# A decode transformer block on one core: coarser score steps, PV first in TensorE's loop, fewer loads at the end, wider down tiles

## The chip, the core and the metric

One core of a Trainium2 chip runs the whole block as one program. The metric is device time in microseconds (us), the median of several executions. The profile is one execution; its span is some 1.2 us shorter than that execution's device time (201.7 against 202.93 before). Engines are written as the profile writes them: PE is TensorE, PEld its weight loads, DVE VectorE, ACT ScalarE, SPq the queue that issues the loads. TensorE's clock is full or half in these traces; "cold" means half.

## The reference, cut to what matters

```python
# x: (1,1,640)  k_cache, v_cache: (1,32,4096,128)  wq: (640,4096)  wo: (4096,640)   all bf16
def A(x):                                  # 32 heads of 128, one query token
    q = (x @ wq) per head
    p = softmax(q . K^T / sqrt(128))       # 4096 keys a head
    return (p . V) @ wo
def B(x):                                  # gated GELU, inner width 1728
    return (gelu(x @ w_gate) * (x @ w_up)) @ w_down
h  = x + A(layernorm(x))
h2 = h + B(layernorm(h))
```

There is one token, so every weight and every cache entry is used once: 84.2 MB must come in from memory for one row of output.

## The kernel before

The heads run in 8 groups of 4. For each group K and V come in as loads of 4 MB. DVE multiplies K by the query, in four steps of 32 rows, TensorE adds up the products over 8 slices of 16 by matmuls with an identity matrix (a "fold"), and DVE adds the last 16 columns in PSUM, the memory that TensorE's results go to in these traces. TensorE's loop puts the product of probabilities and V ("PV") of the group before between the third and the fourth fold:

```python
    def fold(e, i):                        # one step of 32 rows: 8 matmuls of 512 columns into one bank
        for b in range(8):
            mm = held if b else lambda e, *a, **k: e.matmul(*a, **k)
            r = mm(e, ps_f[i % 2][:, :], id_b[:, :], prod[:, i, :, 16 * b:16 * b + 16], start=(b == 0), stop=(b == 7))
    ...
    lp = P.loop("tensor", range(1, NG), [
        ("h", lambda e, k: head_sum(e, k * 4 - 4), lambda k: [evs[k - 2] if k > 1 else qc], False),
        body_fold(0), body_fold(1), body_fold(2),
        ("pv", lambda e, k: pv(e, view(v_slot), range(32)), lambda k: [blocks[k - 1], landed["V"][k - 1][0]], True),
        body_fold(3)])
```

There is one buffer for V, so the next V may be asked for only when PV has read the last. At the end each load is cut so that work can start on its first part:

```python
    wo_load("0", 0, 0, 16)
    wo_load("1a", 1, 0, 12)
    wo_load("1b", 1, 12, 16)
    ...
    proj_part(0, 0, 16, ap, d_wo["0"])     # 160 matmuls of one column in all, in three parts
    proj_part(1, 0, 12, ap, d_wo["1a"])
    pr = proj_part(1, 12, 16, d_wo["1b"])
    ...
    # gate and up: 14 tiles of w, at step 4; the fourteenth has 64 columns
    ws = w[:, c, 512 * (m // 4) + m % 4:512 * (m // 4) + 512:4] if m < 12 else w[:, c, 128 * m:min(128 * m + 128, DF)]
    ...
    # down: four outputs of 160 columns, at partitions 0, 32, 64 and 96
    i = e.matmul(ps_d[32 * q:32 * q + 1, 0:160], h, wd_sb[:, m, n:n + 160], start=False, stop=(m == 11))
```

The softmax here doesn't subtract the row's maximum and nothing guards it: scores larger than these inputs give would overflow.

## Time and profile before

| | before |
|---|---|
| time, median of the first 3 runs | 203.23 us (202.88 to 203.44) |
| span of the profile | 201.7 us |
| moved by the loads | 84.31 MB, mean 418 GB/s |
| PE, DVE busy | 60%, 52% of the span |
| last load landed (trace) | 199.40 us |

### The profile page before, as it was taken

What the parts mean: (1) busy time and instruction counts of PE and PEld (TensorE: products, weight loads), DVE (VectorE), ACT (ScalarE), POOL (GpSimd) and SP (SyncE); (2) the same over time, 40 slices, a digit from 0 to 9 for tenths busy, and PEclk for the clock granted to TensorE, in tenths of its full rate; (3) what the DMA queues carried; (4) which work ended last, traced back from release to release, by engine and by line L of the source; (5) the groups of instructions that cost most, each with busy time, mean ns of one, the idle gap of its engine ahead of it and who ended that gap; (6) DMA issues with size and microseconds to landing.
All of it is one profiled execution on the core that took longest, in us unless ns stands there. A gap on an engine that the chain in (4) does not pass through costs nothing.

```text
span 201.7 us, 2059 instructions
## 1 busy us (share of the span) xinstructions
PE 121.9 (60%) x1002; PEld 36.9 (18%) x778; DVE 105.7 (52%) x114; ACT 12.6 (6%) x33; POOL 2.4 (1%) x8
## 2 busy tenths in 40 slices
PE   0108057759566907880896198528834894777395
PEld 0103000201200300030012001200120013467383
DVE  4200189898189328924890589069707963000221
ACT  2100000000100100010001000100100010100101
POOL 4000000000000000000000000000000000000000
PEclk9999859988979985995589679966985698555555
DMA  9999999999999999999999999999999999999992
GB/s 357 415 398 468 429 422 416 422 442 465 377 455 422 422 422 444 429 455 422 422 422 435 442 429 442 429 422 416 448 429 448 393 432 427 427 408 440 409 411 105
DMA packets 4329, 84.31 MB, mean 418 GB/s; under 512 B 482, under 2 KB 868, under 8 KB 1508
## 3 DMA queue, kind: packets, MB, share of 16 engines
q1 hardware_dynamic: 4322, 84.23, 97.9%
q8 instruction: 4, 0.07, 0.1%
q14 instruction: 1, 0.01, 0.0%
q10 hardware_dynamic: 2, 0.00, 0.0%
HBM read 84.23 MB, written 0.00 MB: 418 GB/s over the span
## 4 chain that ended last, share of the span: by engine, by line
DMA 60%; DVE 20%; PE 11%; SPq 6%; ACT 1%; issue 1%
DMA k_slot<-in_A_k_cache_dram 49%; DVE prod L377 15%; DMA k_slot<-in_B_w_down_dram 11%; SPq L59 6%; PE bank L167 6%; PE bank L353 4%; DVE sc L369 3%; DVE p_bd L394 1%; PE bank L346 1%; ACT pt L392 1%; PE bank L521 0%; DVE out_row L534 0%
## 5 line engine op out<-in xcount | busy, mean ns | idle before, releaser
L377 DVE TENSOR_TENSOR prod<-k_slot,qb 128x4096 bf16<-128x4096 bf16 x32 | 73.0, 2285 | 43.4 <-DMA k_slot<-in_A_k_cache_dram 43.4
L167 PE MATMUL bank<-prod,id_b 128*128 128x512 bf16 x224 | 66.7, 448 | 0.0
L346 PE MATMUL bank<-prod,id_b 128*128 128x512 bf16 x32 | 14.9, 465 | 53.3 <-DVE prod L377 53.0
L369 DVE TENSOR_REDUCE sc<-bank 128x32 f32<-128x512 f32 x32 | 21.9, 686 | 3.8 <-PE bank L167 3.8
L346 PEld LDWEIGHTS bank<-prod,id_b 128*128 128x128 bf16 x32 | 3.1, 98 | 102.5 <-DVE prod L377 99.5
L353 PE MATMUL bank<-v_slot,p_bd 128*16 128x512 bf16 x224 | 13.3, 379 | 0.0
L359 PEld LDWEIGHTS bank<-hs,po_sb 128*128 128x128 f32 x72 | 10.2, 207 | 13.3 <-issue 10.0
L359 PE MATMUL bank<-hs,po_sb 128*128 128x4 f32 x72 | 9.5, 255 | 0.7 <-ACT po_sb L366 0.7
L366 ACT COPY po_sb<-bank 128x512 f32<-128x512 f32 x8 | 4.7, 586 | 73.0 <-PE bank L353 73.0
L332 PE MATMUL bank<-arena,xlnB 128*32 128x512 bf16 x40 | 4.5, 630 | 7.0 <-DMA arena<-in_A_wq_dram 7.0
L491 PE MATMUL bank<-hlnT,v_slot 128*128 128x1 bf16 (+1 forms) x140 | 6.7, 176 | 3.0 <-DMA v_slot<-in_B_w_gate_dram 3.0
L353 PEld LDWEIGHTS bank<-v_slot,p_bd 128*16 128x16 bf16 x224 | 5.0, 89 | 17.6 <-issue 12.8
L394 DVE TENSOR_TENSOR p_bd<-pt,own 128x512 bf16<-128x512 bf16 x8 | 5.5, 693 | 4.5 <-ACT pt L392 4.5
L448 PE MATMUL bank<-aP,arena 128*128 128x1 bf16 x160 | 6.7, 178 | 1.9 <-DMA arena<-in_A_wo_dram 1.9
L392 ACT ACTIVATE pt<-sc,zero_t 128x128 bf16<-128x128 f32 x8 | 3.2, 402 | 71.7 <-DVE sc L369 71.7
L491 PEld LDWEIGHTS bank<-hlnT,v_slot 128*128 128x128 bf16 (+1 forms) x140 | 6.3, 118 | 3.9 <-DVE hX L481 3.1
L448 PEld LDWEIGHTS bank<-aP,arena 128*128 128x128 bf16 x160 | 6.6, 131 | 2.0 <-DMA arena<-in_A_wo_dram 1.3
L336 DVE CAST qb<-bank 128x512 bf16<-128x512 f32 x1 | 0.7, 692 | 10.0 <-PE bank L332 10.0
L306 PE MATMUL bank<-one_bf,x_row 1*128 1x1 bf16 x5 | 0.4, 177 | 7.1 <-DMA x_row<-in_A_x_dram 7.1
L478 DVE TENSOR_TENSOR hT<-xx,bank 128x5 f32<-128x5 f32 x1 | 0.2, 161 | 8.3 <-PE bank L448 8.3
L353 PE MATMUL bank<-k_slot,p_bd 128*16 128x512 bf16 x32 | 2.9, 502 | 1.2 <-DMA k_slot<-in_A_v_cache_dram 1.2
L432 DVE TENSOR_TENSOR aT<-bank,rz 128x32 bf16<-128x32 f32 x1 | 0.2, 192 | 6.3 <-PE bank L359 6.3
(68 smaller groups left out, 28.0 us busy)
## 6 DMA issues: line engine op xcount, KB each, us to landing
k_slot<-in_A_k_cache_dram SPq DMA_DIRECT2D x8, 4096.0 KB, 25.5
v_slot<-in_A_v_cache_dram SPq DMA_DIRECT2D x7, 4096.0 KB, 16.1
arena<-in_A_wq_dram SPq DMA_DIRECT2D x1, 5120.0 KB, 15.4
k_slot<-in_A_v_cache_dram SPq DMA_DIRECT2D x2, 2048.0 KB, 22.9
arena<-in_A_wo_dram SPq DMA_DIRECT2D x1, 2560.0 KB, 30.7
v_slot<-in_B_w_gate_dram SPq DMA_DIRECT2D x1, 2160.0 KB, 24.6
arena<-in_A_wo_dram SPq DMA_DIRECT2D x1, 1920.0 KB, 34.8
v_slot<-in_B_w_up_dram SPq DMA_DIRECT2D x1, 1296.0 KB, 27.3
```

The costliest lines, as they stand in the source:

```text
L59: ev = self.op(eng, lambda e: e.dma_start(out, in_), *deps, dma=True, chan=chan)
L167: built = e.matmul(out, lhsT, rhs, start=start, stop=stop)
L346: mm = held if b else lambda e, *a, **k: e.matmul(*a, **k)
L353: i = e.matmul(ps_o[a:a + 16, :], p_bd[:, 4 * b:4 * b + 4, :].rearrange("p g j -> p (g j)"), vt[:, 4 * b:4 * b + 4, :], start=(b < 4), sto ...
L359: i = e.matmul(ps_a[:, bass.ds(at, 4)], po_sb[:, 128 * r:128 * r + 128], hs[:, r, :], start=(r == 0), stop=(r == 3))
L366: evs[G] = AS(lambda e: e.copy(po_sb[:, :], ps_o[:, :]), pvs[G])
L369: reds[4 * G + i] = VS(lambda e: e.reduce_sum(sc[:, G % 2, 32 * i:32 * i + 32], ps_f[i % 2][:, :].rearrange("p (g d) -> p g d", d=16), axi ...
L377: mults[s] = VS(lambda e, i=i: e.tensor_tensor(out=prod[:, i, :, :], in0=kt[:, 32 * i:32 * i + 32, :], in1=qb[:, G, :].unsqueeze(1).to_bro ...
L392: exps[G] = AS(lambda e: e.activation(pt[:, G % 2, :], sc[:, G % 2, :], ACTF.Exp, bias=zero_t[:, 0:1], scale=INV_SQRT_DH, accum_out=RS[:, ...
L394: blocks[G] = VS(lambda e: e.tensor_tensor(out=p_bd[:, :, :], in0=pt[:, G % 2, :].unsqueeze(2).to_broadcast([128, 128, 4]), in1=own[:, :]. ...
L448: r = e.matmul(ps_p[:, c:c + 1], wo_sb[:, t, i, c::5], aP[:, t, i:i + 1], start=(t == 0 and c == 0 and i == 0), stop=(t == 1 and i == 15), ...
L491: i = e.matmul(ps[0:128 if m < 13 else 64, m:m + 1], ws, hlnT[:, c:c + 1], start=(c == 0 and m == 0), stop=(c == 4), skip_group_check=True)
```

## The change

Its intent is fewer and larger pieces: half as many products, a quarter as many sums, one load each for wo and up, no duplicate selection tables, two output tiles instead of four. The core of the diff, with cuts:

```diff
-    prod = sb("prod", [128, 4, 32, DH], BF16)
+    prod = sb("prod", [128, 2, 64, DH], BF16)
+    ps_f = psum[:, 0:2048]
...
+        reds[G] = VS(lambda e: e.reduce_sum(sc[:, :], ps_f.rearrange("p (g d) -> p g d", d=16), axis=AX.X),
+                     folds[G, 1], exps.get(G - 1))
...
     lp = P.loop("tensor", range(1, NG), [
-        ("h", ...), body_fold(0), body_fold(1), body_fold(2), ("pv", ...), body_fold(3)])
+        ("pv", lambda e, k: pv(e, view(v_slot)), lambda k: [blocks[k - 1], landed["V"][k - 1]], True),
+        body_fold(0), body_fold(1),
+        ("h", lambda e, k: head_sum(e, k * 4 - 4), lambda k: [evs[k - 1]], False)])
...
-    wo_load("0", 0, 0, 16)
-    wo_load("1a", 1, 0, 12)
-    wo_load("1b", 1, 12, 16)
+    d_wo = P.dma("sync", wo_sb[:, :, :], A_wo[:, :].rearrange("(p i) n -> p i n", i=32), qd)
...
-    d_wu = [P.dma("sync", wu_sb[:, 0:3, :], wu_v[:, 0:3, :]),
-            P.dma("sync", wu_sb[:, 3:5, :], wu_v[:, 3:5, :])]
+    d_wu = P.dma("sync", wu_sb, B_w_up[:, :].rearrange("(p c) n -> p c n", c=5))
+    blk = {0: (0, 7), 7: (896, 6)}
...
+                    lo, per = (0, 7) if m < 7 else (896, 6)
+                    at, step = (lo + m - 7 * (m >= 7), per) if m < 13 else (1600, 1)
+                    i = e.matmul(ps[:, m:m + 1], w[:, c, at:at + 127 * step + 1:step], hlnT[:, c:c + 1],
...
+    tiles = ((0, 280), (280, 360))
+                        i = e.matmul(ps_d[32 * t:32 * t + 1, o:o + w], hc, wd_sb[:, m, a:a + w], start=False, stop=(m == 12))
```

Besides these, setup moves from DVE to GpSimd, the Q projection changes its order, the last V comes as one load with its PV in one piece (before, two halves), and x is added to the attention's result by a matmul.

## The prediction

> **What bounds the kernel now.** I read the busy slices of the page first, then the chain that ended last, then the queue's own waits, then the timeline of one group and of the last 32 us.
>
> ```profile
> PEclk9999859988979985995589679966985698555555
> DMA  9999999999999999999999999999999999999992
> ```
>
> The DMA row is full from the first slice to the last but one: 84.31 MB at a mean of 418 GB/s. TensorE is at half clock for the last six slices.
>
> ```profile
> 176.75 22.26 DMA k_slot<-in_B_w_down_dram
> 199.01 0.04 issue
> 199.05 0.74 PE bank L521 x13
> 199.80 0.30 DVE out_row L534
> ```
>
> The chain ends in the last load. Only 2.7 us of the 201.7 follow it, so before is bound by bytes, and TensorE's tail is hidden just barely. The queue's own waits say whether loads are issued late:
>
> ```profile
> SPq L59 <- PE bank L353: 104.1, 6, 18.6
> SPq L59 <- DVE prod L377: 49.9, 2, 34.1
> ```
>
> These waits fill the issuer's time but not the engines': in the timeline of one group
>
> ```profile
> 93.64 2.29 DVE L377 TENSOR_TENSOR prod<-k_slot,qb 128x4096 bf16<-128x4096 bf16 x1 [6.89 <-DMA k_slot<-in_A_k_cache_dram]
> ...
> 104.67 1.90 PE L353 MATMUL bank<-v_slot,p_bd 128*16 128x512 bf16 x32
> ...
> 106.62 0.33 SPq L59 DMA_DIRECT2D v_slot<-in_A_v_cache_dram  x1
> ...
> 113.06 2.29 DVE L377 TENSOR_TENSOR prod<-k_slot,qb 128x4096 bf16<-128x4096 bf16 x1 [6.70 <-DMA k_slot<-in_A_k_cache_dram]
> ```
>
> the next V is issued at 106.62 while the K that lands at 113.06 is still moving: 6.4 us of slack. One group lasts 19.42 us = 8.39 MB at 432 GB/s. The tail, TensorE:
>
> ```profile
> 169.16 1.04 PE L353 MATMUL bank<-k_slot,p_bd 128*16 128x512 bf16 x16
> 171.43 1.89 PE L353 MATMUL bank<-k_slot,p_bd 128*16 128x512 bf16 x16 [1.23 <-DMA k_slot<-in_A_v_cache_dram]
> ...
> 177.63 3.33 PE L448 MATMUL bank<-aP,arena 128*128 128x1 bf16 x80 [0.72 <-DMA arena<-in_A_wo_dram]
> ...
> 182.15 3.36 PE L448 MATMUL bank<-aP,arena 128*128 128x1 bf16 x80 [1.18 <-DMA arena<-in_A_wo_dram]
> ...
> 189.60 3.34 PE L491 MATMUL bank<-hlnT,v_slot 128*128 128x1 bf16 x70 [3.04 <-DMA v_slot<-in_B_w_gate_dram]
> 192.87 0.71 PE L500 MATMUL bank<-hX,ones_f 128*1 128x160 f32 x8
> 193.51 3.37 PE L491 MATMUL bank<-hlnT,v_slot 128*128 128x1 bf16 x70
> 197.33 1.50 PE L521 MATMUL bank<-k_slot,hm 128*1 128x160 bf16 x40
> ```
>
> Every stage waits for its own load and half of the output projection is done before the rest of wo lands. That is why 16 us of TensorE work fit behind the loads.
>
> **What the Trainium skill says.** (1) "DMA: Bandwidth & Descriptors", section "Where 436 GB/s comes from": 435 GB/s is the ceiling of the ports. The trace agrees (432 in the stream), so the stream has nothing to give. (2) "TensorE: Matmul & The Clock Gate", "The HAM clock gate": the clock halves after an idle window of about 3.4 us and comes back after about 3.4 us of activity. The trace agrees in the stream (half clock at the start of each group), but from 189.6 to 196.9 TensorE ran one-column matmuls without a gap and stayed at half clock: such work does not wake it. So I count the tail at half clock. (3) Same page, "Weight-path perf modes": fast weight load needs 128 weight columns. It agrees: equal 0.66 us windows hold 17 matmuls of the projection (40 ns each) but only 14 of the gate, since each 14 of those have one tile of 64 columns; the 13 full tiles come 33 ns apart, so the 64-column one costs some 0.23 us. (4) "SBUF — State Buffer", note on cachelines of 16 bytes: at least two hits per line are needed for full speed. The trace fits: weights at step 4 (two hits) come every 33 ns, at step 5 every 40 ns. In TensorE cycles of 1/1.2 ns that is 40 and 48, so my estimate is 8 + 8 x step: 56 cycles (47 ns) at step 6, 64 (53 ns) at step 7.
>
> **The change, part by part.**
>
> *Stream (K and V).* DVE: four products of 2.20 and four sums of 0.60 a group become two products (2.20 x 2 = 4.4, same rate) and one sum of 2048 columns ((2048/512) x 0.533 + 0.15 = 2.3); 11.9 us a group becomes 11.8, so nothing. What moves is order. PV first means it runs as V lands, 9.7 us after K; in half clock 32 matmuls take 3.6 (16 took 1.89), so V is issued some 13.5 us after K's landing where 13.0 was: slack about 6 us, still no gap. But both folds now stand behind PV: 32 folds of 0.23 us, the first few at 0.43, end 20 to 24 us after K's landing, and sum, exponent and block follow (2.3 + 0.5 + 0.7 + gaps = 3.6). The next group's products slip to 4 to 8 us behind their K, still inside the period of 19.4. The stream stays full: 0 us. Setup moved to GpSimd, and Q projection (pairs in one column group now, up to 9 us for 4.4) end about when the first K lands at 25.1: 0 us.
>
> *End of attention.* K of the last group lands at 151.9. Folds end at 172 to 176 (middle 174), block at 177.5. PV of 32 in one piece 1.9 to 3.6, evacuation 0.7, head sums 1.0 to 1.9, five small steps 1.7: aP ready at 182.6 to 185.2, where it was 177.1. The last V landed at 171.4, and wo's 5.24 MB at 422 GB/s come 12.4 us later, 183.8, now in one load. So the projection starts at about 184.6 (not under 183.9), all 160 matmuls of it: 160 x 0.040 = 6.4. Before, it ended at 185.5; now at 191.2. Lost: 5.7 us. Before had 1.5 us to spare until the gate's load at 189.5, so 4.1 of it comes out as delay there.
>
> *GLU.* Layer norm unchanged (h at 185.54 to first gate matmul possible at 188.0: 2.5). Gate per fifth: 7 x 53 + 6 x 47 + 33 = 0.69 us against 0.66: the 64-column tile goes (-0.2) and the steps 7 and 6 eat it. 3.4 us each for gate and up, about +0.1 each; if steps above 4 cost only 40 ns, 2.6 each, -1.4 in all.
>
> *Residual.* Four column groups of 160 at 4 passes took 0.65 (533 ns + 0.11); two of 280 and 360 take 360 x 4/1.2 = 1.2 + 0.11 = 1.31: +0.66.
>
> *Down.* Four 160-column matmuls side by side came every 133 ns a tile (160/1.2). Two of 280 and 360 take 300 ns. Before, 10 tiles ran from 197.33 and the last four waited for loads; end 199.78. Now all loads (landed by 199.4 as before) are there when the activations are: 14 x 0.30 + 0.24 = 4.4 us, all exposed, against 2.45.
>
> *Output.* One copy of 360 on ACT (0.15 + 360 x 0.85 ns = 0.46) for two of 0.29 in a row (0.62): -0.16.
>
> *Sum, along the new chain:* projection start 184.6; +6.6 to h; +2.5 to gate; +3.3 and 0.14 to the residual; +1.3; +3.2 up; +0.66 to the first down matmul (as before, 196.67 to 197.33); +4.4 to the copy; +0.5; +1.2 to the end of the write (200.5 to 201.7 before). This gives 208.4, against 201.7: +6.7 us. On 203.2 that is 209.9; I take 209.6, since the cheaper GLU would take up to 1.4 off.
>
> **The rivals.** (a) *The loads still end it*: fewer and longer rows (the last slice but three fell to 353 GB/s with 1280-byte rows), one 128-column tile instead of the slow 64-column one, and PV earlier; then nothing moves, 202 to 204. For it: DMA is the bound now. Against: TensorE's tail alone is 24 us from wo's landing (6.6 + 2.5 + 6.9 + 1.3 + 0.7 + 4.4 + 1.7) where the loads leave 15.6. (b) *The stream starves*: the late folds push products and loads so far that the queue runs dry for some us per group; 212 to 220. For it: V's slack is only 6 us, the clock could stay half longer. Against: PV waits for V alone, not for the folds. (c) *Clock*: PV, folds and down keep TensorE warm into the tail; the down stage and the GLU then cost half, 205 to 207. Against: no wake-up from one-column work before. (d) *Folds of the last group all cold*: they end at 179, aP near 190, 214 to 215.
>
> **Range and chances.** Start of projection 183.9 to 186, GLU 2.6 to 3.5 each: 206.9 to 211.5 in time; some weight for (b) and (d) puts the top at 212.0, for (c) the bottom at 207.0. The 2% line is 207.3. Faster by over 2% would need 4 us from a stream at the ports' ceiling: 1%. Within 2%: 13%. Slower: 86%.
>
> **What would show it.** DMA slices still 9 until about 199, then zeros for about 9 us (right) or zeros inside the stream (rival b). The chain should end in TensorE lines: projection, gate, residual, up, down, with no wait for B's loads. Projection near 184.6 and 6.4 long; gate windows at 46 to 54 ns a matmul; down at 300 ns a tile. If the chain still ends in in_B_w_down_dram, or the projection starts before 183.8, I am wrong on the tail; if the clock row shows full speed after 185, on the clock.

## The result, and the profile after

| | before | after |
|---|---|---|
| time, median of 4 runs each, same rounds | 203.33 us (202.88 to 203.64) | 208.92 us (208.54 to 209.06) |
| ratio, with 95% interval | | 1.0274 (1.0249 to 1.0298) |
| span | 201.7 us | 207.3 us |
| packets | 4329 | 3609 |
| last load landed (trace) | 199.40 us | 199.25 us |

A ratio here is the mean time of a kernel's fast runs over that of the other's of the same rounds, so it is not quite the ratio of the medians. The change is slower by 2.7%, close to the 209.6 us predicted.

The busy slices of the page after, to be held against the two rows of before:

```profile
PEclk9999857958965995599559958965896589675557
DMA  9899999999999999999999999999999998999900
```

The loads run as densely as before and stop 8 us before the end (199.25 of 207.3) instead of 2.3. The stream did not slow down; the engines were left behind it. The last part of the chain that ended last (start, duration, what):

```profile
146.89 36.81 DMA arena<-in_A_wo_dram
183.70 0.14 issue
183.84 6.55 PE psum L431 x160
...
192.93 3.57 PE psum L447 x70
196.50 1.30 PE psum L457 x4
197.79 3.51 PE psum L447 x70
...
201.81 3.75 PE psum L482 x25
205.56 0.02 issue
205.58 0.45 ACT out_row L494
```

Before, this chain ended in a load of down weights at 199.0. Now the last load on it is wo, at 183.7, and then come projection (L431), gate (L447), residual (L457), up (L447) and down (L482) one behind the other, none waiting for a load. One group of the stream, from the timeline:

```profile
98.77 8.76 DVE L356 TENSOR_TENSOR prod<-k_slot,qb 128x8192 bf16<-128x8192 bf16 x2
103.55 3.59 PE L343 MATMUL psum<-v_slot,p_bd 128*16 128x512 bf16 x32 [7.49 <-DMA v_slot<-in_A_v_cache_dram]
...
107.19 0.33 SPq L59 DMA_DIRECT2D v_slot<-in_A_v_cache_dram  x1
...
115.26 2.29 DVE L365 TENSOR_REDUCE sc<-psum 128x128 f32<-128x2048 f32 x1 [7.73 <-PE psum L167]
```

PV now runs when V lands (103.55) and cold: 3.59 us for 32 matmuls (1.90 at full clock before). V is asked for at 107.19, while the K that lands at 113.22 is under way: 6.0 us of slack, where before had 6.4. The sum comes 21.5 us after its K landed (93.80 in the trace), as late as expected, and still the loads have no gap. The end of attention, from the same view:

```profile
177.01 3.13 PE L343 MATMUL psum<-k_slot,p_bd 128*16 128x512 bf16 x32 [2.85 <-DVE p_bd L369]
...
183.16 0.19 DVE L406 CAST aP<-psum 128x32 bf16<-128x32 f32 x1 [0.28 <-PE psum L404]
...
183.84 6.53 PE L431 MATMUL psum<-aP,arena 128*128 128x1 bf16 x160 [0.50 <-DMA arena<-in_A_wo_dram]
```

Two things come together at 183.8 in this execution: the attention output aP is ready at 183.35 (177.13 before), and the one load of wo lands at 183.70. Either alone would have stopped the early start of the projection. That they meet within 0.4 us is this execution's: in the profiles of e4, e5 and e6, which leave this part as it is, aP was ready 0.5 to 1.5 us before the load landed. This pair is what the experiments had to take apart.

### The profile page after: what moved, and what is told of

Same layout as the page of the kernel before. It is cut to its first block, busy times and chain, and to the rows that moved or that the text cites. A ratio compares the mean times of both kernels' runs of the same rounds, so it can differ in the third digit from the quotient of the medians.

```text
span 207.3 us, 1891 instructions
## 1 busy us (share of the span) xinstructions
PE 122.0 (59%) x964; PEld 36.8 (18%) x704; DVE 101.3 (49%) x63; ACT 12.4 (6%) x32; POOL 2.1 (1%) x13
## 2 busy tenths in 40 slices
DMA packets 3609, 84.31 MB, mean 407 GB/s; under 512 B 402, under 2 KB 660, under 8 KB 916
## 4 chain that ended last, share of the span: by engine, by line
DMA 77%; PE 20%; DVE 1%; issue 1%; SPq 1%; ACT 1%; DVEq 0%
DMA v_slot<-in_A_v_cache_dram 59%; DMA arena<-in_A_wo_dram 18%; PE psum L343 10%; PE psum L447 3%; PE psum L431 3%; PE psum L482 2%; PE psum L457 1%; SPq L59 1%; PE psum L301 0%; ACT out_row L494 0%; ACT ln L306 0%; ACT ln L305 0%; DVE hlnT L435 0%; DVE ln L303 0%; PE psum L485 0%
## 5 line engine op out<-in xcount | busy, mean ns | idle before, releaser
L356 DVE TENSOR_TENSOR prod<-k_slot,qb 128x8192 bf16<-128x8192 bf16 x16 | 70.0, 4419 | 4.4 <-DMA k_slot<-in_A_k_cache_dram 4.4
L167 PE MATMUL psum<-prod,id_b 128*128 128x512 bf16 x240 | 58.8, 400 | 0.0
L343 PE MATMUL psum<-v_slot,p_bd 128*16 128x512 bf16 x224 | 25.0, 626 | 52.7 <-DMA v_slot<-in_A_v_cache_dram 52.7
L365 DVE TENSOR_REDUCE sc<-psum 128x128 f32<-128x2048 f32 x8 | 18.3, 2292 | 54.1 <-PE psum L167 54.1
L343 PEld LDWEIGHTS psum<-v_slot,p_bd 128*16 128x16 bf16 x224 | 6.9, 124 | 68.7 <-DMA v_slot<-in_A_v_cache_dram 56.9
L336 PE MATMUL psum<-prod,id_b 128*128 128x512 bf16 x16 | 7.3, 454 | 9.6 <-DVE prod L356 9.6
L349 PEld LDWEIGHTS psum<-hs,po_sb 128*128 128x128 f32 x64 | 8.4, 192 | 23.9 <-issue 23.5
L447 PE MATMUL psum<-hlnT,v_slot 128*128 128x1 bf16 x140 | 7.1, 188 | 1.5 <-DVE hlnT L435 1.5
L349 PE MATMUL psum<-hs,po_sb 128*128 128x4 f32 x64 | 7.8, 244 | 0.1
L447 PEld LDWEIGHTS psum<-hlnT,v_slot 128*128 128x128 bf16 x140 | 7.0, 146 | 2.8 <-DVE hlnT L435 1.6
L431 PE MATMUL psum<-aP,arena 128*128 128x1 bf16 x160 | 6.5, 178 | 0.5 <-DMA arena<-in_A_wo_dram 0.5
L431 PEld LDWEIGHTS psum<-aP,arena 128*128 128x128 bf16 x160 | 6.5, 131 | 0.6 <-DVE aP L406 0.6
L482 PE MATMUL psum<-k_slot,hm 128*1 128x280 bf16 (+3 forms) x29 | 3.8, 431 | 0.0
```

Source lines behind the costliest of these rows:

```text
L167: built = e.matmul(out, lhsT, rhs, start=start, stop=stop)
L343: i = e.matmul(ps_o[a:a + 16, :], p_bd[:, 4 * b:4 * b + 4, :].rearrange("p g j -> p (g j)"), vt[:, 4 * b:4 * b + 4, :], start=(b < 4), sto ...
L349: i = e.matmul(ps_a[:, bass.ds(at, 4)], po_sb[:, 128 * r:128 * r + 128], hs[:, r, :], start=(r == 0), stop=(r == 3))
L356: mults[G, i] = VS(lambda e, i=i: e.tensor_tensor(out=prod[:, i, :, :], in0=kt[:, 64 * i:64 * i + 64, :], in1=qb[:, G, :].unsqueeze(1).to_ ...
L365: reds[G] = VS(lambda e: e.reduce_sum(sc[:, :], ps_f.rearrange("p (g d) -> p g d", d=16), axis=AX.X), folds[G, 1], exps.get(G - 1))
L431: r = e.matmul(ps_p[:, c:c + 1], wo_sb[:, i, c::5], aP[:, i:i + 1], start=False, stop=(i == 31), skip_group_check=True)
```

## The experiments

The theory: the stream is unharmed and the 5.6 us come from TensorE's tail behind wo, where every term now counts in full: all of the projection (two gates side by side, the single load and the late aP), the gate and up stages (the weight columns' steps 7 and 6), residual and down (two tiles for four). The rivals: one of the two gates alone, the loads of the tail, or a stream that is delayed by the score steps. Twelve kernels were run, five rounds each except one. "Points" below are percentage points of the ratio to before; one point is 2.03 us. A "gate" here is a wait that holds the projection back; the stage with the weights w_gate is called the gate stage. Where PV comes last, executions differ by more than elsewhere, and a ratio's interval is about 0.25 to 0.5 points to each side.

### e1_wo_parts: open the gate of the load

```diff
-    d_wo = P.dma("sync", wo_sb[:, :, :], A_wo ..., qd)
+    wo_parts = ((0, 16), (16, 28), (28, 32))
+    d_wo = [P.dma("sync", wo_sb[:, lo:hi, :], wo_v[:, lo:hi, :], qd) for lo, hi in wo_parts]
+    for (lo, hi), d in zip(wo_parts, d_wo):
+        pr = proj(lo, hi, ap, d)
```

> The changed kernel with the output projection's weights in three loads (half, three eighths, one eighth) and the projection cut to match; PV stays first in the loop. Theory (two gates side by side: the one load lands at 183.8, but the attention output is ready only at 183.35 because PV stands ahead of the folds): the projection can start only 0.4 us earlier, so 208.5, -0.4 us. Rival (the single load alone is what delays the projection): the first two parts are done under the last load and the time drops by 3 to 4 us, to 205 to 206.

Measured: 208.28 us, ratio 1.0237, so 0.37 points or 0.75 us faster than the changed kernel (0.1 to 1.4 us by the two intervals); the span fell by 0.5. The theory held, the rival did not. The projection starts as soon as aP is there, and all 160 matmuls follow without a wait:

```profile
183.27 6.56 PE L433 MATMUL psum<-aP,arena 128*128 128x1 bf16 x160
```

### e2_pv_last, e3_both and e7_three: open the other gate by moving PV behind the folds

```diff
     lp = P.loop("tensor", range(1, NG), [
-        ("pv", ...),
         body_fold(0), body_fold(1),
+        ("pv", ...),
         ("h", ...)])
```

e3_both adds the three loads of e1_wo_parts, and e7_three the four tiles of e4_down4 as well.

> The changed kernel with PV after both folds in TensorE's loop; the weights of the projection stay one load. Theory: the attention output is ready near 177 instead of 183.35, but the projection still waits for the one load at 183.8: no change, 208.9 within 0.3. Rival (PV first alone is the cause): 3 to 4 us faster, 205 to 206.

> The changed kernel with both edits, the three loads and PV last. Theory: both gates open, the projection ends near 185.5 and the gate projection starts when its own weights land, near 189.1 instead of 192.9: -3.8 us, 205.1. That is far more than the sum of the two single edits (-0.4). Rival (the two are additive): -0.4 or less if both singles do little.

> The changed kernel with the three loads, PV last, and the four-tile residual, down and output: still score steps of 64 rows, one sum over 4 banks, blocks of 7 and 6. Theory: the tail hides behind the loads again, the last load lands at about 199.2 and the time is that of the kernel before, 203.1 within 0.4; the parts left (64 rows, one sum, 7 and 6) cost nothing while the loads are the bound. Rival (the score steps or the sum delay the stream): 204.5 or more.

Measured: 215.16 us (1.0580), 212.59 us (1.0449) and 211.98 us (1.0382). All three expectations missed on the level: the edit itself costs over 6 us. The DMA row of e2_pv_last's page and its queue's timeline say why:

```profile
DMA  9899999998389999999999999999999999989920
```

```profile
56.95 0.33 SPq L59 DMA_DIRECT2D v_slot<-in_A_v_cache_dram  x1
```

The second V was asked for at 48.09 in the changed kernel and is asked for at 56.95 here, because PV of the first group now stands behind both folds of the second. The K under way had landed at 54.4 and the queue ran dry: the next V landed 4.4 us later than in the changed kernel (69.06 against 64.65), and the last V 5.1 later. So the "PV first" of the change is not an ornament: with steps of 64 rows it is what keeps the loads without a gap. I had counted that part as 0 us, which was its net worth in the change, but the change without it would have been far worse.

The comparison of e2 with e3, which share the gap, still tests the gates. In e2 TensorE waits 5.70 us for the one load with its inputs ready:

```profile
188.95 6.21 PE L431 MATMUL psum<-aP,arena 128*128 128x1 bf16 x152 [5.70 <-DMA arena<-in_A_wo_dram]
```

and cutting the load then gives 1.31 points, 2.7 us, where with PV first it gave 0.75. The traces also show what PV's place does to aP: it was ready 6.5 to 7.7 us after the last V landed in the six kernels with PV last, 10.7 to 11.8 us after it in the changed kernel and the other four with PV first, and 5.8 in the kernel before.

### e4_down4: residual, down and output in four tiles

```diff
-    tiles = ((0, 280), (280, 360))
+    tiles = ((0, 160), (160, 160), (320, 160), (480, 160))
...
-    dn = [T(down([12], [t]), d_wd[3]) for t in range(2)]
+    dn = {t: T(down([12], [t]), d_wd[3]) for t in (0, 2, 1, 3)}
```

> The changed kernel with residual, down projection and output copies in four column tiles of 160 again. Theory (TensorE's tail is the path, each of its terms counts in full): residual 1.31 to 0.65, down 3.80 to 2.07, copies 0.45 to 0.62: -2.2 us, 206.7. Rival (the loads of the down weights or the fixed cost of the write end the kernel): no change, 208.9.

Measured: 206.34 us, ratio 1.0149, 1.25 points or 2.5 us faster than the changed kernel; the span fell by 2.2. In the timeline the residual and the down stage take

```profile
196.43 0.71 PE L457 MATMUL psum<-hX,ones_f 128*1 128x160 f32 x8
...
201.09 2.09 PE L482 MATMUL psum<-k_slot,hm 128*1 128x160 bf16 x56
```

against 1.37 and 3.81 in the changed kernel. In the trace of e4 the four tiles of 160 run side by side: their starts are up to 7 ns apart, and a set of four comes every 133 ns, where two tiles took 300 at half clock. Once the tail is exposed, that is worth its full time.

### e5_steps: what the step between weight columns costs

Gate and up read their 128 weight columns at ten different steps.

```diff
+    STEPS = ((1, 2, 3, 4, 5), (6, 7, 8, 10, 13))
...
+                    at, step = 0, STEPS[ps is ps_u][c]
```

> Wrong result on purpose: the changed kernel whose gate and up matmuls read their weight columns at steps 1, 2, 3, 4, 5 (gate, one step for each of the five row groups) and 6, 7, 8, 10, 13 (up), 14 matmuls each. Theory (cost of a 128-column weight load is 8 + 8 x step cycles of 1/1.2 ns with a floor near 25 to 33 ns): 33 ns at step 4, 40 at 5, 47 at 6, 53 at 7, 60 at 8, 73 at 10, 93 at 13. Rival (a line of 16 bytes is the unit, so past step 8 every column has its own line): 60 at 8 and no more at 10 and 13.

The time between the starts of neighbouring matmuls, inside each 14 of one step, from the records of the trace (one execution without rounds, its state unknown, this stretch at half clock):

| step | 1 | 2 | 3 | 4 | 5 | 6 | 7 | 8 | 10 | 13 |
|---|---|---|---|---|---|---|---|---|---|---|
| ns a matmul | 26.7 | 26.7 | 28 | 33 | 40 | 46.7 | 53.3 | 62 | 62 | 60 |

From 4 to 7 the rule of the theory, 8 + 8 x step cycles of 1/1.2 ns, holds to the nanosecond. From 8 on the rival, with a line of 16 bytes as the unit, is right: the cost stays at 60 to 62. Blocks of 7 and 6 pay 53 and 47 of these 62.

### e6_glu4: gate, up and down in blocks of 4

```diff
-                    lo, per = (0, 7) if m < 7 else (896, 6)
-                    at, step = (lo + m - 7 * (m >= 7), per) if m < 13 else (1600, 1)
+                    at, step = (512 * (m // 4) + m % 4, 4) if m < 12 else (1536, 1) if m == 12 else (1600, 1)
```

The loads of the down weights are those of before.

> The changed kernel with gate, up and down in blocks of 4 tiles as before (steps 4 and 1), the fourteenth tile 128 columns wide as in the changed kernel. Theory: 70 matmuls at 33 ns or less, 2.3 us each instead of 3.5: -2.3 us, 206.6. Rival (the step costs nothing of itself and the last tile's width was all): no change, 208.9.

Measured: 206.82 us, ratio 1.0172, 1.02 points or 2.1 us faster. The theory held:

```profile
192.89 2.40 PE L444 MATMUL psum<-hlnT,v_slot 128*128 128x1 bf16 x70 [1.49 <-DVE hlnT L433]
...
199.41 4.36 PE L479 MATMUL psum<-k_slot,hm 128*1 128x280 bf16 x29
```

Gate takes 2.40 instead of 3.57. The down stage gave 0.5 back: it took 4.36 instead of 3.81, because here its last matmul started (203.27) before the clock rose (203.67; see below). The kernel has both good things, the step of 4 and the full fourteenth tile; neither of the two kernels has both. So most of the 2.1 us is not a loss against before, where gate and up took 3.34 and 3.37 (3.57 and 3.56 in the changed kernel).

### e8_before_full13: the same gain where it is hidden

```diff
-                        w[:, c, 128 * m:min(128 * m + 128, DF)]
-                    i = e.matmul(ps[0:128 if m < 13 else 64, m:m + 1], ws, ...
+                        w[:, c, min(128 * m, DF - 128):min(128 * m + 128, DF)]
+                    i = e.matmul(ps[:, m:m + 1], ws, ...
```

> The kernel before with one edit: its fourteenth gate and up tile reads 128 columns (64 of them twice) instead of 64. Theory: the gate and up stages lose about 1.0 us each on TensorE (66 to 47 ns a matmul on average), but the last load ends the kernel: 203.3, change under 0.4 us. Rival (TensorE's tail is part of the bound in the kernel before): about -2 us, 201.4.

Measured: 203.23 us, ratio 0.9993 (0.9974 to 1.0013): nothing. Gate fell from 3.34 to 2.40 us, and TensorE then waited for loads instead, the last time just before the end:

```profile
195.03 0.61 PE L489 MATMUL bank<-hlnT,v_slot 128*128 128x1 bf16 x14 [0.59 <-DMA v_slot<-in_B_w_up_dram]
...
199.35 0.70 PE L519 MATMUL bank<-k_slot,hm 128*1 128x160 bf16 x16 [0.46 <-DMA k_slot<-in_B_w_down_dram]
```

A microsecond on TensorE is worth a microsecond in e6_glu4 and nothing here. This is the plainest sign that the bound moved from the loads to the tail.

### e10_before_wo_all: close the gate in the kernel before

```diff
-    proj_part(0, 0, 16, ap, d_wo["0"])
+    proj_part(0, 0, 16, ap, d_wo["0"], d_wo["1a"], d_wo["1b"])
```

> The kernel before with one edit: its projection waits for all three of its loads before the first matmul, as if they were one. Theory: projection from 183.9 instead of 177.6, gate from 193.0 instead of 189.6, and all after it exposed: down ends at 202.8 instead of 199.8, so +3.0 us, 206.4. Rival (a late projection is made good under the loads): 203.5 to 204.

Measured: 206.04 us, ratio 1.0135, 2.7 us slower. From the timeline:

```profile
183.99 6.53 PE L448 MATMUL bank<-aP,arena 128*128 128x1 bf16 x160 [6.91 <-DMA arena<-in_A_wo_dram]
```

TensorE sat idle for 6.91 us, 6.7 of them with aP ready, and the late projection was not made good. So one closed gate alone, in the kernel before, costs half of what the change lost.

### e11_peel, e12_peel_wo and e13_peel_wo_down4: PV last, without its first gap

```diff
+    pvs[0] = T(lambda e: pv(e, view(v_slot)), blocks[0], landed["V"][0])
+    scores(1)                                # first pass out of the loop, PV first
+    lp = P.loop("tensor", range(2, NG), [ body_fold(0), body_fold(1), ("pv", ...), ("h", ...)])
```

e12 adds the three loads, e13 the four tiles too.

> PV last again, but the first pass of TensorE's loop is taken out of it and keeps PV first, so that the second V is asked for at 48 as in the changed kernel and not at 57. One load of the projection's weights. Theory: no gap in the loads, the attention output is ready near 178, and the projection still waits for the one load at 183.8: 208.9 within 0.4. Rival (PV first in the tail is by itself a cause of the loss): 205 to 206. Second rival (PV last starves the loads in every pass, not in the first alone): 212 or more.

> The same with the projection's weights in three loads. Theory (two gates side by side, so opening both pays what neither pays alone): the gate matmuls start when their own weights land, near 189.1 instead of 192.9: -3.8 us, 205.1. Rival (additive): the sum of the two single edits, 208.3.

> The same with residual, down and output in four tiles as well; score steps of 64 rows, one sum over 4 banks and blocks of 7 and 6 stay. Theory: the tail hides behind the loads again and the last load ends the kernel: 203.3 within 0.4, the time of the kernel before; what is left of the change costs nothing there. Rival (the parts left cost something of themselves): 204.3 or more.

Measured: 213.62 us (1.0518), 210.20 us (1.0343) and 208.23 us (1.0212). The levels missed again: the gap moved from the second pass to the third (V asked for at 74.61 instead of 68.33, the last V 3.5 us later than in the changed kernel). The second rival of e11 was right on the level, but its "in every pass" is not what the trace shows: the queue ran dry in one pass (73.97 to 75.56), and in the later ones V was asked for 3.6 to 5.1 us before the K under way landed.

The pairs again tell the gates apart. In e11 aP is ready and the one load holds TensorE back:

```profile
187.31 5.33 PE L440 MATMUL psum<-aP,arena 128*128 128x1 bf16 x130 [4.40 <-DMA arena<-in_A_wo_dram]
```

In e12 the projection runs in parts as its loads land, and the gate stage waits for its own load, as in the kernel before:

```profile
186.40 3.36 PE L442 MATMUL psum<-aP,arena 128*128 128x1 bf16 x80 [1.18 <-DMA arena<-in_A_wo_dram]
...
193.41 3.54 PE L460 MATMUL psum<-hlnT,v_slot 128*128 128x1 bf16 x70 [2.59 <-DMA v_slot<-in_B_w_gate_dram]
```

From e11 to e12 the time fell by 1.75 points, 3.6 us. (In e11's profile TensorE also paused for 1.17 us inside the projection, put down to issue; I have no cause for that; a fetch of 16 KB of instructions ran from 191.3 to 192.4, just before the pause, but nothing ties the two. The rounds, not this profile, give the 3.6.) The same edit gave 0.75 with PV first. That is the interaction which the theory asked for, near the 3.8 expected, though in kernels whose loads are some 3.5 us late.

e13 is still 2.1% over before. Its last load landed at 204.16 in the trace, 4.8 later than before. The last V was already 3.6 later (174.94 against 171.38); of the rest, 1.0 arose while wo came in, 13.5 us after the last V instead of 12.5, and I have not found its cause. Its chain ends in up, which is one load of which all must be there:

```profile
171.78 27.30 DMA v_slot<-in_B_w_up_dram
```

No run here has both an early aP and loads without a gap. A kernel that keeps PV first in every pass but the last would be the next to try; it was not run. Whether all parts of the change that are left (steps of 64 rows, one sum, blocks of 7 and 6) cost nothing while the loads are the bound therefore stays open. None of the runs is faster than the kernel before beyond its interval.

## Why the prediction was right

The forecast was 209.6 us; 208.92 was measured. By its own steps, in spans:

- **Stream, 0 us: right.** Last V at 171.51 (171.4 said), wo at 183.70 (183.8), V asked for 13.4 us after its K (13.5), folds of a group ended 21.4 us after it (20 to 24). What the step did not see is that the order of PV was needed for this 0: e2, e3, e7, e11, e12 and e13 all starved without it. The rival of a starved stream was listed with the folds as its cause, and set aside since PV waits for V alone; that holds just as long as PV comes first.
- **Q projection, "up to 9 us for 4.4": too careful.** In the trace four matmuls still start within 40 ns of each other: first to last start 15.5 to 19.3, as before. No effect either way.
- **Start of the projection, 184.6: off by 0.8, mechanism right.** aP was ready at 183.35, inside the 182.6 to 185.2, so wo's load set the start, 183.84. The lower end named, 183.9, was the value. (The steps listed for aP add up to 182.8 to 185.4; the 182.6 to 185.2 written is a slip of 0.2.) Two gates side by side, as said; e1, e10, e12 against e11 show both.
- **Projection 6.6, layer norm 2.5: right** (183.84 to 190.41, then to 192.93).
- **Gate and up, 47 and 53 ns at steps 6 and 7: right** (46.7 and 53.3). The estimate from two points, 33 at step 4 and 40 at step 5, was good between 4 and 7, and e5 shows that it ends at 8. The alternative of 40 ns for all steps fell; its 2.6 us a stage is a slip too, as five times 13 x 40 + 33 ns is 2.8. That two hits a line at step 4 mean full speed did not hold: steps 1 and 2 took 26.7.
- **Residual 1.31: right** (196.43 to 197.72 is 1.29).
- **Down 4.4 to the copy: 3.84.** The step that failed in size is "So I count the tail at half clock". The windows of the changed kernel over the down stage show it (bounds, length, busy and counts of PE, PEld, DVE and ACT, then granted clock, DMA share and GB/s):

```profile
201.73:204.75 3.02, 3.02 (x27) 2.11 (x27) 0.16 (x1) 0.00 (x0) 0.50 0.02 5
204.75:205.55 0.80, 0.79 (x7) 0.24 (x3) 0.11 (x1) 0.00 (x0) 0.94 0.00 0
```

  The clock rose 3.1 us into the stage (at 204.84), for its last 0.7 us. In that stretch the tile of 360 came every 153 ns instead of 300. Rival (c) of the prediction was right in this one part, though for gate and up (the GLU of the prediction) it is not shown that a higher clock would have helped: the one-column projection took 40 ns a matmul at full and at half clock alike. Where the rise falls is luck: in the seven other kernels with two tiles it came 2.7 to 4.8 us after the stage began, and the stage took 3.60 to 4.36 us.
- **Copy and write, 0.5 and 1.2: right** (0.45; 206.12 to 207.3).

Sum: 208.4 said, 207.3 measured; the 0.8 of the start and the 0.6 of the clock are the difference, with 0.2 the other way in the steps between. The 0.3 us then taken off for a cheaper GLU brought the forecast nearer for a reason that fell, which is luck. Two readings were off: not every stage waited for its own load, since up (193.51) shows no such wait; and the 353 GB/s are the two microseconds from 196 to 198, not a slice of the page.

Where the 5.6 us lie is seen from the two timelines: the gate stage starts 3.3 us later (192.93 against 189.60), the down stage 4.4 (201.74 against 197.33), and the output is issued 5.6 later (206.12 against 200.50). So 3.3 come from the late projection, 1.1 from gate, residual and up, and 1.2 from down and its copies. What undoing gives back (four tiles 2.5, the step of 4 with a full last tile 2.1, both gates some 3.6 where the loads are late anyway) does not add up to the loss, since before had up to 1.5 us to spare at the gate stage, e6 is faster than before in gate and up, and in before the last load ends the kernel even when TensorE gets faster, as e8 shows.

## What to carry to other kernels

In a kernel bound by loads, ask of each merged load and each coarser step which work could start on its first part, and count the engines' time from the last wait to the end: as long as that fits under the remaining loads it costs nothing, and beyond that it counts, as e8 and e6 show with the same kind of edit. Where two waits end at the same moment, undoing one alone shows little (0.75 us here), so test them as a pair. The order of an engine's work also sets when a buffer comes free: PV first looked idle in the sum and kept the loads without a gap.

## What the Trainium skill lacked or had wrong

- "SBUF — State Buffer", the note on cachelines: it calls a step of up to 8 bf16 elements free. For loads of 128 weight columns on TensorE the runs show 26.7 ns at steps 1 and 2, 33 at 4, 40, 46.7 and 53.3 at 5, 6 and 7, and 60 to 62 from 8 on (e5, at half clock). Its unit of 16 bytes fits the end of the rise at 8; its range without cost does not.
- "TensorE: Matmul & The Clock Gate", "Weight-path perf modes": fast weight load needs 128 columns, which agrees, but there is no figure for one short tile in a stream of full ones. Here a tile of 64 columns among 13 full ones cost about 0.23 us against 0.033, and reading 64 columns twice to fill it took gate from 3.34 to 2.40 us.
- Same page, "The HAM clock gate": it does not say whether matmuls of one column count as activity. Matmuls of one column, back to back from 189.6 to 196.9 in the kernel before, left the clock at half; in the changed kernel and the seven others with two tiles the clock rose 2.7 to 4.8 us after the start of the down stage, whose matmuls have one weight column and 280 or 360 streamed columns. The one-column projection of the changed kernel kept its 40 ns both in its first 0.5 us, at full clock, and after that at half.
